# Sparse attention and a squared-ReLU MLP on one core: the second batch's loads reordered on GpSimd's queue, and a mask tile for the first batch

## The chip, the cores and the metric

The kernel runs on 1 core of one Trainium2 chip. The metric is the device time of one execution in microseconds (us). TensorE (PE) multiplies, VectorE (DVE), ScalarE (ACT) and GpSimd (POOL) work on tiles, SyncE (SP) issues transfers. Transfers issued by GpSimd and by SyncE go through two queues of descriptors to the same DMA engines.

## The reference, cut to what matters

q, k and v are [8 batches, 8 heads, 576 positions, 64]. The first four heads of each batch use a local mask, the last four a strided one; the output of attention, 4608 tokens of 512, goes through an MLP.

```python
scores = (q @ k^T) / 8
mask_local   = (rel >= 0) & (rel < 32)                         # heads 0..3, rel = i - j
mask_strided = (rel >= 0) & (pos_j % 32 == pos_i % 32)         # heads 4..7
attn = softmax(where(mask, scores, -1e9)) @ v
x = attn as [4608, 512]
out = (max(x @ w_in, 0) ** 2) @ w_out                          # w_in [512, 2048], w_out [2048, 512]
```

## The kernel before, in words

**Units and chunks.** Two heads of one batch make a unit: unit u = 4·batch + pair, pairs 0 and 1 local, 2 and 3 strided. The MLP works on chunks of 512 tokens. A chunk has 16 first matmul groups (`mm1`, L440, "MM1": four 128x512 matmuls at L448, ReLU on ScalarE at L454, square on VectorE at L455) and 16 second groups (`mm2`, L459, "MM2": four matmuls at L466). MM2 of a chunk runs over quarters of w_out: the first groups use only rows of the first quarter, `w_out(0)`, then three need `w_out(1)`, and so on.

**Steps of a unit.** `step_T` (L236) transposes q and k on TensorE (six matmuls for a local unit, eight for a strided one) and copies the result out of PSUM. `step_S` (L271) makes scores, exponentials on ScalarE (L299) and multiplications with the mask on VectorE (L305). `step_D` (L375) multiplies with v and divides by the sum of the exponentials (L406, L407). `step_E` (L410) transposes the result into `xt`, the input of MM1. From batch 2 on some of these transposes are made by DMA (`transpose_str` L158, `transpose_local` L165, L417), issued by SyncE.

**Batch 0** is written out by hand in `first_steps` (L496): a list of T, S, M (masks), N (sums and their reciprocals, L341 to L344), O (product with v), X (scaling into `xt`, L371) and P (parts of the first three MM1 groups); a number in the list is that many idle matmuls (L491). The local mask is one [128, 96] tile, broadcast over six blocks; the first block of units 0 and 1 has 32 rows set to zero by a memset (L307) after each multiplication. For strided units X reads and writes in the order (p, j).

**From batch 1 on** a planner lays attention steps among the MLP's groups. Groups have numbers (MM1 of chunk 0 is 0 to 15, MM2 of chunk 0 is 16 to 31, and so on) and weights (MM1 3, MM2 7 in the first chunks, L665 to L668). Between `g_prev` and `g_end` a batch's steps come due in proportion to the weights passed (L714 to L723). For batch 1 `g_prev` is 12 (L717) and `g_end` is 31. The attention of batch 1 has to be done before MM1 of chunk 1.

**Loads of batches 1 to 3**: `loads` (L563). SyncE's queue gets q and k of the two local units (L113), then v of all four (L185, L201). GpSimd's queue, in the order of the program, gets transfers and casts mixed. For batch 1: w_out(0), strided q and k of unit 6 (cast in the transfer, L133), casts of q and k of unit 4 (L123), w_out(1), casts of unit 5, strided q and k of unit 7, w_out(2), casts of v of the local units (L192, L193), w_out(3), casts of v of the strided units (L208). GpSimd runs these in that order, and a cast waits for SyncE's load of its source.

**Gates.** The first load of batch 1 and of batch 2 writes a tile that GpSimd first touches with a one-element copy (L112) from a weight tile (`gates`, L561): for batch 1 from the third quarter of w_in, for batch 2 from the third quarter of w_out. So SyncE starts batch 2's loads once w_out(2) has landed and GpSimd has come to that copy, behind its casts of batch 1. SyncE's queue is in program order as well.

Of the kernel before, what the change touches and what calls it, by code (L numbers as in the profile page):

```python
# [8 lines left out]
FP32 = mybir.dt.float32  # L9
BF16 = mybir.dt.bfloat16  # L10
AF = mybir.ActivationFunctionType
ALU = mybir.AluOpType

@with_exitstack
def kernel(
# [9 lines left out]
    nc = tc.nc  # L25
    B, H, S, D = q.shape
    d_model, d_ff = moe_w_in.shape
    T = B * S
# [3 lines left out]
    QL = 96  # L32
    NL = S // QL
    NJ = 8
    RH = STRIDE // NJ
    SP_ = RH * NA
# [13 lines left out]
    y_pool = ctx.enter_context(tc.tile_pool(name="y_pool", bufs=4))  # L50
# [12 lines left out]
    mask_loc = singles.tile([128, 1, QL], BF16)  # L63
    mask_str = singles.tile([SP_, 1, SP_], BF16)
# [5 lines left out]
    xt = [singles.tile([128, T], BF16, name=f"xt{p}") for p in range(4)]  # L70
# [56 lines left out]
    def load_qk_str(u):  # L127
        b, p = units[u]
        s = st.setdefault(u, {})
        for name, src in (("q", q), ("k", k)):  # L130
            t = strT.tile([128, NJ // 2, 4 * SP_], BF16, name=f"{name}T_s")
            t = t.rearrange("p a c -> p (a c)")[0:SP_, 0:2 * NJ * D].rearrange("p (h c) -> p h c", h=2)
            nc.gpsimd.dma_start(out=t, in_=src[b, 2 * p:2 * p + 2]  # L133
                                .rearrange("h (p j) d -> p h (j d)", j=NJ))
            s[name] = t
# [11 lines left out]
    XB = 2  # L147
# [67 lines left out]
    def load_w_out(i):  # L215
        c = slice(4 * i, 4 * (i + 1))
        nc.gpsimd.dma_start(out=w_out_b[:, c, :], in_=w_out_v[:, c, :])
# [53 lines left out]
    def step_S(u):  # L271
        s = st[u]
        qT, kT = s["qT"], s["kT"]
        local = is_local(u)
        w, n = (QL, NL) if local else (SP_, NJ)
        kn = 128 if local else SP_
        hn = n // 2
        e = es[u % 4]
        s["e"] = e
        banks = [[None, None], [None, None]]  # L280
        for half in range(2):
            for row in range(2):
                banks[row][half] = ps_t.tile([128, 512], FP32, name="pt")
            for i in range(hn):
                t = half * hn + i
                klo = w * t
                for row in range(2):
                    rows = slice(64 * row, 64 * row + 64)
                    if not local and units[u][0] >= XB:
                        c0 = w * (t // 4)  # L290
                        lhsT, rhs = (a[rows, t % 4, c0:c0 + w] for a in (kT, qT))
                    else:
                        lhsT, rhs = kT[rows, klo:klo + kn], qT[rows, w * t:w * (t + 1)]
                    nc.tensor.matmul(banks[row][half][0:kn, w * i:w * (i + 1)], lhsT, rhs,  # L294
                                     start=True, stop=True)

        def expo(row, half):
            lo = S * row + S // 2 * half
            nc.scalar.activation(e[0:kn, lo:lo + S // 2], banks[row][half][0:kn, 0:S // 2],  # L299
                                 AF.Exp, scale=scale)  # L300

        def masks(row):
            x = e[0:kn, S * row:S * (row + 1)].rearrange("p (t c) -> p t c", c=w)
            m = mask_loc if local else mask_str
            nc.vector.tensor_tensor(x, x, m.to_broadcast([kn, n, w]), op=ALU.mult)  # L305
            if u < 2:
                nc.vector.memset(x[0:32, 0], 0.0)  # L307

        s["masks"] = masks
        if units[u][0] == 0:  # L310
            for row, half in ((0, 0), (0, 1), (1, 0), (1, 1)):
                expo(row, half)
            return
        expo(0, 0)
        later(1, lambda: expo(0, 1), u)
        later(2, lambda: (masks(0), expo(1, 0)), u)
        later(3, lambda: expo(1, 1), u)
        later(4, lambda: masks(1), u)

    def load_v_first():  # L320
# [25 lines left out]
    def step_O(u):  # L346
        s = st.pop(u)
        e, local, i = s["e"], is_local(u), u % 2
        kn, w, hw = (128, QL, S // 2) if local else (SP_, SP_, S // 2)
        pos = []  # L350
        for half in range(2):
            po = ps_t.tile([128, 512], FP32, name="pt")
            for t in range(hw // w):
                for h in range(2):
                    if local:
                        tt = NL // 2 * half + t
                        vt, c = vl0[:, i, h, tt], S * h + w * tt
                    else:
                        vt, c = vs0[:, i, NJ * h + 2 * t + half], S * half + hw * h + w * t
                    nc.tensor.matmul(po[64 * h:64 * h + 64, w * t:w * (t + 1)], vt, e[0:kn, c:c + w],  # L360
                                     start=True, stop=True)
            pos.append(po)

        def scaled():
            for half, po in enumerate(pos):
                cols = slice(hw * half, hw * (half + 1))
                o, x, r = xt[u][:, cols], po[:, 0:hw], rv0[:, u, cols]
                if not local:
                    o = xt[u][:, 0:S].rearrange("c (p j r) -> c p j r", j=NJ // 2, r=2)[:, :, :, half]
                    x, r = (y.rearrange("c (j p) -> c p j", p=SP_) for y in (x, r))  # L370
                nc.vector.tensor_tensor(o, x, r, op=ALU.mult)  # L371

        return scaled
# [108 lines left out]
    D_ = lambda u, part: (lambda: step_D(u, part))  # L482
    E_ = lambda u: (lambda: step_E(u))

    idle_w = y_pool.tile([128, 512], FP32, name="y").bitcast(BF16)

    def warm(n):
# [8 lines left out]
    def first_steps():  # L496
        a, b, c, d = first_order
        scaled = {}

        def part(kks, ffs=range(NP)):  # L500
            for ff in ffs:
                mm1(0, ff, kks, (b, a, c, d), None if ff < 2 else ps_y)

        def masks(u):
            for row in range(2):
                st[u]["masks"](row)

        def outs(u):
            scaled[u] = step_O(u)

        for item in (("T", a, "q"), 2, ("T", a, "k"), 2, ("T", b, "q"), ("S", a), 1, ("T", b, "k"), 2, ("S", b),
                     ("M", a), 1, ("T", c, "q"), ("T", c, "k"), 1, ("N", a), ("S", c), 1, ("M", b), ("N", b), 1,
                     ("T", d, "q"), ("T", d, "k"), 2, ("S", d), 1, ("M", c), ("N", c), ("O", b), 1, ("X", b),
                     ("O", a), 1, ("M", d), ("X", a), ("N", d), ("O", c), ("X", c), ("P", (b, a), (0,)), ("O", d),
                     ("P", (b, a), (1, 2)), ("X", d), ("P", (c,)), ("P", (d,))):
            if isinstance(item, int):
                warm(item)
                continue
            op, u = item[0:2]
            if op == "T":  # L520
                step_T(u, item[2])
            elif op == "S":
                step_S(u)
            elif op == "M":
                masks(u)
            elif op == "N":
                step_N(u)
            elif op == "O":
                outs(u)
            elif op == "X":  # L530
                scaled[u]()
            else:
                part(*item[1:])
# [29 lines left out]
    def loads(b):  # L563
        u = 4 * b
        for i in range(2):
            load_qk_local(u + i, nc.sync, gate=gates.get(b) if i == 0 else None)
        for i in range(2):
            load_v_local(u + i, nc.sync)
        load_v_str(u + 2, nc.sync)
        load_v_str(u + 3, nc.sync)  # L570
        w_out = load_w_out if b == 1 else (lambda i: None)
        if b >= XB:
            cast_str_dram(b)
        w_out(0)
        if b < XB:
            load_qk_str(u + 2)
        cast_qk_local(u, pool2)
        w_out(1)
        cast_qk_local(u + 1, pool2)
        if b < XB:  # L580
            load_qk_str(u + 3)
        w_out(2)
        cast_v_local(u)
        cast_v_local(u + 1)
        w_out(3)
        cast_v_str(u + 2)
        cast_v_str(u + 3)

# [104 lines left out]
    done_prev, g_prev = 0, 0  # L693
# [20 lines left out]
    for b in range(1, B):  # L714
        g_end, s_end = ready.get(b, starts[b] - 2), ends[4 * b + 3]
        if b == 1:
            g_prev = 12  # L717
        total = sum(weights[g_prev:g_end])
        for g in range(g_prev, g_end + 1):
            due[g] = done_prev + (s_end - done_prev) * sum(weights[g_prev:g]) // total  # L720
        if b + 2 < B:
            plan(b + 2, g_end + 2, g_prev, g_end)
        done_prev, g_prev = s_end, g_end  # L723
# [41 lines left out]
```

## Time and profile before

| What | Value |
|---|---|
| Time, median of 13 runs | 317.89 us (316.56 to 319.82) |
| The profiled execution's own time | 317.94 us |
| Its span | 315.3 us |
| TensorE busy | 303.2 us (96%) |
| VectorE, ScalarE, GpSimd busy | 167.6, 162.7, 89.0 us |
| DMA | 44.4 MB, mean 141 GB/s |
| w_out, four transfers, issue to landing | 8.7 to 11.0 us |
| MM1 of chunk 0 without breaks (L448) | from 23.93 us |
| MM2 of chunk 0 (L466) | 35.67 to 61.07 us |
| TensorE's waits up to 110 us | 1.5 us for kTl copies, 1.5 us for w_out, smaller ones |

Times are counted from the start of the span; the 2.6 us between span and time lie around it. A row of a timeline has a start, a length, the engine (SPq is SyncE's queue of transfers), the line, the operation, what is written and read, the count, and in brackets how long the engine was idle before and what ended that. PEclk in the page is the clock granted to TensorE, in tenths of full speed.

### The profile page before, as it was taken

How to read it: one execution, taken by the hardware profiler on the slowest of the kernel's cores; microseconds unless marked ns; L12 is line 12 of the kernel's file. 1: busy time of each engine (PE TensorE's matmuls, PEld its weight loads, DVE VectorE, ACT ScalarE, POOL GpSimd, SP SyncE). 2: the span in 40 equal slices, each digit the busy share in tenths (PEclk: the TensorE clock that was granted, in tenths of full speed). 3: DMA queues.
4: the chain of work that ended last, by engine and by line, in shares of the span. 5: the costliest groups of instructions: out<-in, count | busy, mean ns of one | idle time of the engine just before them, and what ended most of it. 6: DMA issues, size and time to landing. Idle time of an engine off the chain costs nothing.

```text
span 315.3 us, 6218 instructions
## 1 busy us (share of the span) xinstructions
PE 303.2 (96%) x2384; PEld 149.5 (47%) x2384; DVE 167.6 (53%) x415; ACT 162.7 (52%) x337; POOL 89.0 (28%) x115
## 2 busy tenths in 40 slices
PE   7889979899999999999999999999999999999995
PEld 3444545545555544444444444444454444444442
DVE  6765544568866875577466657565455222222200
ACT  4937636578556765555555555545543444344311
POOL 8524852644840624272048015000000000000000
PEclk9979979999999999999999999999999999999999
DMA  7999999999999999999799876002111100000121
GB/s 147 148 207 223 224 202 210 208 282 217 192 216 212 175 200 205 174 239 224 143 231 222 174 160 119 33 33 54 52 45 45 45 35 34 33 35 33 51 82 67
DMA packets 86612, 44.40 MB, mean 141 GB/s; under 512 B 71032, under 2 KB 79896, under 8 KB 86392
## 3 DMA queue, kind: packets, MB, share of 16 engines
q1 hardware_dynamic: 77032, 34.09, 50.9%
q0 software_dynamic: 9408, 9.80, 19.8%
q8 instruction: 18, 0.29, 0.4%
q10 hardware_dynamic: 144, 0.13, 0.1%
q14 instruction: 10, 0.08, 0.1%
HBM read 36.70 MB, written 12.98 MB: 158 GB/s over the span
## 4 chain that ended last, share of the span: by engine, by line
PE 77%; DMA 10%; DVE 6%; SPq 3%; ACT 1%; issue 1%; POOL 1%; DVEq 0%; POOLq 0%
PE ph L448 32%; PE py L466 27%; PE ph L466 7%; DMA q_st<-in_q_dram 4%; DMA w_out_b<-in_moe_w_out_dram 3%; PE pt L294 3%; PE pt L392 3%; DMA kTl<-k_l 2%; DVE x_s L407 2%; DMA v_st<-in_v_dram 1%; PE pt L424 1%; DVE kTl L265 1%; DVE e L305 1%; PE pt L250 1%; ACT r L454 1%
## 5 line engine op out<-in xcount | busy, mean ns | idle before, releaser
L448 PE MATMUL ph<-xt,w_in_b 128*128 128x512 bf16 x572 | 144.4, 381 | 0.3 <-ACT r L454 0.3
L454 ACT ACTIVATE r<-ph 128x512 bf16<-128x512 f32 x143 | 85.3, 597 | 98.5 <-PE ph L448 97.3
L455 DVE TENSOR_TENSOR g_sb<-r 128x512 bf16<-128x512 bf16 x144 | 68.4, 477 | 104.8 <-ACT r L454 104.1
L466 PE MATMUL py<-w_out_b,g_sb 128*128 128x512 bf16 x400 | 102.8, 379 | 0.0
L466 PEld LDWEIGHTS <-g_sb 128*128 128x128 bf16 x576 | 53.1, 98 | 58.5 <-issue 2.4
L448 PEld LDWEIGHTS <-w_in_b 128*128 128x128 bf16 x576 | 51.8, 98 | 54.5 <-issue 1.0
L299 ACT ACTIVATE e<-pt 128x288 bf16<-128x288 f32 (+1 forms) x128 | 47.2, 407 | 14.5 <-PE pt L294 14.4
L466 PE MATMUL ph<-w_out_b,g_sb 128*128 128x512 bf16 x176 | 44.2, 388 | 1.5 <-DMA w_out_b<-in_moe_w_out_dram 1.5
L392 PEld LDWEIGHTS <-e 128*128 128x128 bf16 (+1 forms) x392 | 21.0, 98 | 15.7 <-issue 0.6
L192 POOL CAST vl<-vl_st 128x768 bf16<-128x768 f32 x14 | 12.6, 899 | 52.4 <-DMA vl_st<-in_v_dram 46.4
L407 DVE TENSOR_TENSOR x_s<-pt,rinv 72x384 bf16<-72x384 f32 (+1 forms) x42 | 21.4, 509 | 1.4
L123 POOL CAST q_l<-q_st 96x768 bf16<-96x768 f32 x14 | 12.5, 894 | 24.3 <-DMA q_st<-in_q_dram 24.0
L305 DVE TENSOR_TENSOR e<-e,mask_loc 128x576 bf16<-128x576 bf16 x32 | 17.5, 548 | 2.4 <-ACT e L299 2.4
L406 DVE RECIPROCAL rinv<-pt 96x6 f32<-96x6 f32 (+2 forms) x70 | 12.9, 184 | 9.0 <-PE pt L392 9.0
L305 DVE TENSOR_TENSOR e<-e,mask_str 72x576 bf16<-72x576 bf16 x32 | 16.3, 513 | 2.0 <-ACT e L299 2.0
L208 POOL CAST vs<-v_st 72x1024 bf16<-72x1024 f32 x14 | 16.3, 1181 | 3.3 <-DMA v_st<-in_v_dram 2.8
L123 POOL CAST k_l<-k_st 96x768 bf16<-96x768 f32 x14 | 13.2, 941 | 13.9 <-DMA k_st<-in_k_dram 9.1
L477 ACT COPY y<-py 128x512 f32<-128x512 f32 x25 | 14.6, 585 | 4.4 <-PE py L466 4.3
L407 DVE TENSOR_TENSOR x_l<-pt,rinv 96x384 bf16<-96x384 f32 x28 | 15.5, 553 | 1.0
L477 ACT COPY y<-ph 128x512 f32<-128x512 f32 x10 | 5.9, 585 | 17.4 <-PE ph L466 17.4
L392 PE MATMUL pt<-vs,e 72*128 72x65 bf16 x224 | 13.1, 193 | 0.0
L193 POOL CAST vl<-vl_st 32x640 bf16<-32x640 f32 x14 | 10.8, 769 | 0.9
(84 smaller groups left out, 157.6 us busy)
## 6 DMA issues: line engine op xcount, KB each, us to landing
out_dram<-y SPq DMA_DIRECT2D x35, 256.0 KB, 2.0
vl_st<-in_v_dram SPq DMA_DIRECT2D x28, 144.0 KB, 5.5
v_st<-in_v_dram SPq DMA_DIRECT2D x14, 288.0 KB
q_st<-in_q_dram SPq DMA_DIRECT2D x16, 144.0 KB, 5.4
k_st<-in_k_dram SPq DMA_DIRECT2D x16, 144.0 KB, 6.6
w_in_b<-in_moe_w_in_dram POOLq DMA_DIRECT2D x4, 512.0 KB, 12.2
w_out_b<-in_moe_w_out_dram POOLq DMA_DIRECT2D x4, 512.0 KB, 9.6
q_st<-in_q_dram SPq DMA_DIRECT2D x7, 288.0 KB, 8.5
```

Of the source, the lines that this page charges most:

```text
L123: copy(t.rearrange("p j h d -> p h j d"), s[name + "f"].rearrange("p h (j d) -> p h j d", j=6))
L208: (copy or nc.gpsimd.tensor_copy)(t[:, :, 0:D], s["vf"].rearrange("p h (j d) -> p (h j) d", d=D))
L299: nc.scalar.activation(e[0:kn, lo:lo + S // 2], banks[row][half][0:kn, 0:S // 2], AF.Exp, scale=scale)
L305: nc.vector.tensor_tensor(x, x, m.to_broadcast([kn, n, w]), op=ALU.mult)
L392: nc.tensor.matmul(po[:, n - n0, :], e[0:kn, pos(n):pos(n) + 128], rhs[0:kn, src(n), 0:D + 1], start=True, stop=True)
L406: nc.vector.reciprocal(rinv[0:w, 0:m], po[0:w, 0:m, D:D + 1])
L407: nc.vector.tensor_tensor(x, po[0:w, 0:m, 0:D], rinv[0:w, 0:m].to_broadcast([w, m, D]), op=ALU.mult)
L448: nc.tensor.matmul(ph, w_in_b[:, kk, 128 * ff:128 * (ff + 1)], xt[kk][:, 512 * c:512 * (c + 1)], start=(kk == order[0]), stop=(kk == order ...
L454: nc.scalar.activation(r, ph, AF.Relu)
L455: later(1, lambda: nc.vector.tensor_tensor(g[:, ff, :], r, r, op=ALU.mult))
L466: nc.tensor.matmul(py, g[:, ff, 128 * j:128 * (j + 1)], w_out_b[:, ff, :], start=(ff == 0), stop=(ff == 15))
L477: nc.scalar.copy(y, py)
```

## The change

1. `loads`, batch 1 only: all four pieces of w_out and both strided pairs are enqueued on GpSimd ahead of every cast, in the order w_out(0), unit 6, w_out(1), w_out(2), unit 7, w_out(3). The order among the casts, SyncE's order and batches 2 and 3 stay.
2. The planner starts batch 1's attention at group 16, the first of MM2(0), instead of group 12. `g_end` stays 31.
3. `first_steps`: a tile `mask_l0` of [128, 6, 96] with the 32 rows of the first block at zero is made once by a copy and a memset on VectorE ("Z" in the list, between scores(a) and the k transposes of b), and units 0 and 1 multiply with it; their four memsets go. It takes one more of the four buffers of `y_pool`.
4. `first_steps`: the sums of b (N) come after the transposes of d instead of before them; the idle matmuls around are split anew, with the same total.
5. X of the strided units runs in the order (j, p): PSUM and the reciprocals are read contiguously, and `xt` is written with a step of eight elements.

```diff
         def masks(row):
             x = e[0:kn, S * row:S * (row + 1)].rearrange("p (t c) -> p t c", c=w)
-            m = mask_loc if local else mask_str
-            nc.vector.tensor_tensor(x, x, m.to_broadcast([kn, n, w]), op=ALU.mult)
+            m = (mask_loc if local else mask_str).to_broadcast([kn, n, w])
             if u < 2:
-                nc.vector.memset(x[0:32, 0], 0.0)
+                m = mask_l0
+            nc.vector.tensor_tensor(x, x, m, op=ALU.mult)
...
                 if not local:
-                    o = xt[u][:, 0:S].rearrange("c (p j r) -> c p j r", j=NJ // 2, r=2)[:, :, :, half]
-                    x, r = (y.rearrange("c (j p) -> c p j", p=SP_) for y in (x, r))
+                    o = xt[u][:, 0:S].rearrange("c (p j r) -> c j p r", j=NJ // 2, r=2)[:, :, :, half]
+                    x, r = (y.rearrange("c (j p) -> c j p", p=SP_) for y in (x, r))
...
+    mask_l0 = y_pool.tile([128, 512], FP32, name="y").bitcast(BF16)[:, 0:S].rearrange("p (t c) -> p t c", c=QL)
+
+    def make_mask_l0():
+        nc.vector.tensor_copy(mask_l0, mask_loc.to_broadcast([128, NL, QL]))
+        nc.vector.memset(mask_l0[0:32, 0], 0.0)
...
-        for item in (("T", a, "q"), 2, ("T", a, "k"), 2, ("T", b, "q"), ("S", a), 1, ("T", b, "k"), 2, ("S", b),
-                     ("M", a), 1, ("T", c, "q"), ("T", c, "k"), 1, ("N", a), ("S", c), 1, ("M", b), ("N", b), 1,
-                     ("T", d, "q"), ("T", d, "k"), 2, ("S", d), 1, ("M", c), ("N", c), ("O", b), 1, ("X", b),
+        for item in (("T", a, "q"), 2, ("T", a, "k"), 2, ("T", b, "q"), ("S", a), 1, ("Z",), ("T", b, "k"), 2, ("S", b),
+                     ("M", a), 1, ("T", c, "q"), ("T", c, "k"), 1, ("N", a), ("S", c), 1, ("M", b),
+                     ("T", d, "q"), ("T", d, "k"), 1, ("N", b), 2, ("S", d), 1, ("M", c), ("N", c), ("O", b), 1, ("X", b),
...
-        w_out = load_w_out if b == 1 else (lambda i: None)
-        if b >= XB:
+        if b == 1:
+            load_w_out(0)
+            load_qk_str(u + 2)
+            load_w_out(1)
+            load_w_out(2)
+            load_qk_str(u + 3)
+            load_w_out(3)
+        else:
             cast_str_dram(b)
-        w_out(0)
-        if b < XB:
-            load_qk_str(u + 2)
         cast_qk_local(u, pool2)
-        w_out(1)
         cast_qk_local(u + 1, pool2)
-        if b < XB:
-            load_qk_str(u + 3)
-        w_out(2)
         cast_v_local(u)
         cast_v_local(u + 1)
-        w_out(3)
...
         if b == 1:
-            g_prev = 12
+            g_prev = 16
```

More of the change, by code (lines that the diff above doesn't have):

```diff
@@ L518, in first_steps @@
                 continue
-            op, u = item[0:2]
-            if op == "T":
+            op, u = (item + (None,))[0:2]
+            if op == "Z":
+                make_mask_l0()
+            elif op == "T":
                 step_T(u, item[2])
```

## The prediction, made before the changed kernel ran

> **What bounds the kernel now.** I read the busy lines of the page first, then the chain that ended last, then the waits of TensorE, then the rows of GpSimd, SyncE and TensorE in order of time where that chain leaves TensorE. The busy lines, 40 slices of 7.9 us:
>
> ```profile
> span 315.3 us, 6218 instructions
> ...
> PE   7889979899999999999999999999999999999995
> ...
> PEclk9979979999999999999999999999999999999999
> DMA  7999999999999999999799876002111100000121
> ```
>
> TensorE (PE) is full from slice 9 on. Its holes are in slices 1 to 8, and the DMA engines are full from slice 2 to about slice 20. So the early stage is a race between TensorE and the transfers. What GpSimd (POOL) issues there:
>
> ```profile
> 23.66 0.18 POOL L112 CAST q_st<-w_in_b 1x1 f32<-1x1 bf16 x1 [5.79 <-DMA w_in_b<-in_moe_w_in_dram]
> 23.90 0.76 POOL L217 DMA_DIRECT2D w_out_b<-in_moe_w_out_dram  x1
> ...
> 31.86 0.78 POOL L217 DMA_DIRECT2D w_out_b<-in_moe_w_out_dram  x1
> ...
> 35.48 0.68 POOL L133 DMA_DIRECT2D qT_s<-in_q_dram  x1
> ...
> 36.83 0.78 POOL L217 DMA_DIRECT2D w_out_b<-in_moe_w_out_dram  x1
> ...
> 41.12 0.77 POOL L217 DMA_DIRECT2D w_out_b<-in_moe_w_out_dram  x1
> ...
> 44.52 1.26 POOL L208 CAST vs<-v_st 72x1024 bf16<-72x1024 f32 x1 [0.63 <-DMA v_st<-in_v_dram]
> 47.88 0.18 POOL L112 CAST q_st<-w_out_b 1x1 f32<-1x1 bf16 x1 [2.09 <-DMA w_out_b<-in_moe_w_out_dram]
> ```
>
> The four pieces of w_out go out 8.0, 5.0 and 4.3 us apart, because each stands behind casts that wait for their own loads. The last line is the gate of batch 2's loads: it waits for the third piece. TensorE meets the second and the third piece here:
>
> ```profile
> 41.83 1.55 PE L466 MATMUL ph<-w_out_b,g_sb 128*128 128x512 bf16 x4 [1.21 <-DMA w_out_b<-in_moe_w_out_dram]
> ...
> 47.87 1.02 PE L466 MATMUL ph<-w_out_b,g_sb 128*128 128x512 bf16 x4 [0.24 <-DMA w_out_b<-in_moe_w_out_dram]
> ...
> 112.73 0.43 PE L294 MATMUL pt<-kT,kTl 64*128 64x96 bf16 x12 [0.63 <-DMA kTl<-k_l]
> ```
>
> The third line matters as much. It is scores(17), and it waits for a transpose that SyncE (SP) issued at 106.58. In SP's rows, from the gate's release
>
> ```profile
> 48.08 0.32 SPq L113 DMA_DIRECT2D q_st<-in_q_dram  x1
> ...
> 106.58 3.15 SPq L173 DMA_TRANSPOSE kTl<-k_l  x1
> ```
>
> to that one, issues stand end to end with gaps of 0.2 us at most, so a second chain runs beside TensorE from 47.88 to 112.68. Scores(16) at 103.03 was held by its transpose too (1.1 us of weight-load wait). After 113 no TensorE wait names a DMA.
>
> **What the Trainium skill says.** "DMA: Bandwidth & Descriptors", section "Issuing engines are not separate DMA queues": transfers started by different engines run on the same 16 DMA engines and interleave. The trace agrees: counting its packet records by queue, GpSimd's 1 KB packets run at about 195 a us alone (45 to 47 us) and 119 beside SP's 1.5 KB ones (28 to 30 us). Same page, "Queues, rings and completion order": an engine takes turns between rings packet by packet. So a piece enqueued earlier takes its share from SP's loads; bandwidth is not made. Same page, "Anatomy of one DMA — SWDGE (gpsimd) path": waits happen on the issuing sequencer, before dispatch. The 8.0 us between the first two pieces are such waits. "TensorE: Matmul & The Clock Gate", Part 1: after an idle window of about 3.4 us the clock is halved. The trace has granted clock 0.72 in 40 to 45 and 0.94 in 45 to 50, which is 1.7 us of lost clock.
>
> **The change, part by part.**
>
> *Order of GpSimd's queue in batch 1.* Issue times are 0.76, then 0.70 + 0.69, 0.78, 0.78, 0.68 + 0.67, 0.77, together 5.8 us, so all lie between 23.90 and 29.7. The waits these DMAs carry are for transfers landed by 27.5 (the fourth w_in piece: 11.24 + 16.3), and so cost nothing. What is queued behind them is the first q cast, 28.35 to 29.7. The k cast waits for its load until 30.98 anyway, and the 3.7 us of issue that stood between the later casts are gone, so no cast but the first is later for this.
>
> *w_out(1)*. Before, w_out(0) and the strided pair (800 packets) were through at about 33.5, and then GpSimd's queue ran nearly empty from 34.0 to 36.0 (42 packets against some 200). With the piece queued since 26 that dip goes: 160 packets at 100 to 200 a us are 0.8 to 1.6 us. Landing 41.8 becomes about 40.5. TensorE reaches it earlier: 13 groups of first matmuls at 0.865 from 23.93 end at 35.2; with 0.6 for batch 0 (below) 34.6. Three groups at 0.87, four transposes at 0.26 and scores at 0.36 follow, so it asks at 38.6 and stalls 1.9 us (1.2 before).
>
> *w_out(2)* stands ahead of the strided pair of unit 7 now: 288 packets fewer in front, 1.5 us at 190 a us to 3 at 95, beside the 0.8 to 1.6 above. Against that SP's queue now shares in 34 to 36. From 47.8 I take 45.4 (43.3 to 47). TensorE asks at 40.5 + 2.6 + 1.25 for attention = 44.4 and stalls 1.0. From there the old trace needs 61.32 − 47.87 = 13.45 to the next MM1; scores(6) and one transpose now lie behind the point, 0.66. Arrival 59.5, against 61.32: TensorE gains 1.8. The strided pair of unit 7 lands near 46.7, asked for at 46.9; w_out(3) near 49.5 against 49.7. Both are tight.
>
> *The gate* is released by the later of w_out(2) and the last v cast. SP's v loads (2304 packets of 256 bytes) had the DMA engines to themselves in 34 to 36, 1483 packets in 2 us. With GpSimd's queue full I give them 1 us more: last v load near 45.3, cast 1.26, gate 46.6, against 47.88. Bounds: 45.8 (as before) and 49.7 (rival D). So SP's chain starts 1.3 us earlier. w_out(3) has some 140 packets more to go then than before (0.7 us of work), but the DMA engines had spare time after the gate (share 0.90 in 48 to 52), so I charge 0.2: 1.1 us is left at scores(17).
>
> *Attention from MM2(0) on* (the 12 becomes 16) moves two transposes and their copies out of the last MM1 groups and packs the same steps into groups of weight 105 instead of 117 in the planner. TensorE work is the same. Of the tail, where before stalled on x_s four times (1.1 us in all), the order is almost unchanged: nothing, within ±0.5.
>
> *Batch 0.* Four memsets go (0.10 each, and the next matmul waited for the last: 0.5 at 18.40). A copy and a memset come in, into VectorE's 0.71 us hole before 8.04. The copy is bounded by 0.15 (four elements a cycle, "VectorE: DVE Perf Modes", "Mode 4×_2P") and 0.60 (one, "Mode 1× (REGULAR)"); I take 0.3. The strided outputs at L371 took 0.60 against 0.39 for the local ones; reading straight and writing with gaps saves between 0 and 0.2 each, or loses 0.1. The transposes of unit 1 come 0.7 earlier, but ScalarE is busy without a break from 10.5 to 16.9, so that is hidden. Sum 0.3 to 0.9, taken as 0.6, and hidden too: it lengthens the stall for w_out(1). If w_out(1) came by 38.6, it would count.
>
> **The sum.** TensorE is 1.8 earlier at 61, but scores(17) may start only 1.1 earlier; the remaining 0.7 turns into a longer wait there or at scores(16). The profiled run took 317.94, its span 315.3 and 2.6 around it; the median is 317.89, so they agree. 317.9 − 1.1 = 316.8.
>
> **The rivals.**
> B, SP's chain is not rigid: its issues speed up when TensorE does, or the gate comes 2.2 earlier. For it: transposes there took up to 3.15 where 1.22 is usual. Against: 65 us end to end. It gives 317.9 − 2.2 = 315.7.
> C, nothing moves: the clock halves again behind the new stalls (1.7 lost of 1.8) or the last v load holds the gate at 47.9. Then only w_out moved: 317.9. For it: the DMA engines were full anyway.
> D, slower: GpSimd's queue, full from 24 to 48, starves SP's small packets. In 36.5 to 37.0 they stood 113 to GpSimd's 64; at 226 a us their 2304 packets take 10 us instead of 5.2. Some 0.9 of the 4.8 comes back, as GpSimd's queue is then emptier; the last v load lands at 48.4, the gate falls to 49.7, and scores(17) to 112.7 + 1.8: 319.7. It decides once the v_st loads end over 1.3 us later than before. Against: the ratio comes from engines that had finished their SP share.
>
> **Numbers.** About 0.3% (0.95 us) is what can be told from no change. Likeliest case A 0.45 (315.9 to 317.4), B 0.20, C 0.17, D 0.18. Of A 0.27 lies below 316.9 and 0.18 within; with B that is 0.47 faster; C and 0.18 give 0.35 the same; D 0.18 slower. The range 315.2 to 319.3 reaches into B and D and leaves out about 0.15.
>
> **What would show it.** Right: four w_out issues within 6 us, the gate cast (L112) near 46.6, TensorE's wait for w_out near 1.9 and 1.0, and a wait on kTl near 112 that is longer than 0.63. Wrong: a gate after 47.9, v_st casts over 1.3 us late, a wait for w_out(3) or the strided pair, a second half-clock window that reaches past 50, or new waits of batch 2 between 57 and 80.

## The result, and the profile after

The changed kernel takes 322.14 us (median of 11 runs, 321.31 to 324.38), the kernel before 318.42 in the same comparison: ratio 1.0133, interval 1.0107 to 1.0158. It is slower by about 4 us, beyond the forecast range. Ratios here and below leave out executions that were markedly slower than the others of the same kernel, and in two of the experiments (old_queue, start16_only) the profiled execution was such a one, with TensorE's clock halved over 10.2 us, so its times behind that point are not compared.

The page's busy lines of the changed kernel, 40 slices of 8.0 us:

```profile
span 318.2 us, 6217 instructions
...
PE   7979979889999989999999999999999999999995
...
PEclk9969999999999999999999999999999999999999
DMA  8999993998999999999899999002100100000121
```

The seventh digit of the DMA line is new: a 3 stands where a 9 stood. It is the stretch around 50 us. GpSimd's rows there, the same lines as in the prediction:

```profile
22.76 0.18 POOL L112 CAST q_st<-w_in_b 1x1 f32<-1x1 bf16 x1 [6.00 <-DMA w_in_b<-in_moe_w_in_dram]
22.99 0.75 POOL L217 DMA_DIRECT2D w_out_b<-in_moe_w_out_dram  x1
...
25.12 1.53 POOL L217 DMA_DIRECT2D w_out_b<-in_moe_w_out_dram  x2
...
28.00 0.80 POOL L217 DMA_DIRECT2D w_out_b<-in_moe_w_out_dram  x1
...
42.03 0.99 POOL L192 CAST vl<-vl_st 128x768 bf16<-128x768 f32 x1 [6.37 <-DMA vl_st<-in_v_dram]
43.09 0.71 POOL L193 CAST vl<-vl_st 32x640 bf16<-32x640 f32 x1
46.89 1.07 POOL L192 CAST vl<-vl_st 128x768 bf16<-128x768 f32 x1 [3.08 <-DMA vl_st<-in_v_dram]
48.02 0.86 POOL L193 CAST vl<-vl_st 32x640 bf16<-32x640 f32 x1
48.94 2.13 POOL L208 CAST vs<-v_st 72x1024 bf16<-72x1024 f32 x2
51.03 0.40 POOL L112 CAST q_st<-w_out_b 1x1 f32<-1x1 bf16 x1
```

The four pieces of w_out go out within 5.8 us, as foretold. The local v loads then keep GpSimd waiting 6.37 and 3.08 us, the last four v casts stand in a row from 46.89 to 51.0, and only then comes the gate (last line), with no wait of its own: the piece that it needs had landed at 40.6. Before, the gate came at 47.88 and waited for w_out. TensorE's rows that answer to those shown before, with the new wait at 45.88, and SyncE's:

```profile
45.88 0.20 PE L392 MATMUL pt<-vl,e 128*128 128x65 bf16 x1 [1.39 <-DVE e L307]
...
105.50 0.43 PE L294 MATMUL pt<-qT,kTl 64*128 64x96 bf16 x12 [0.36 <-DMA kTl<-k_l]
115.62 0.43 PE L294 MATMUL pt<-kT,kTl 64*128 64x96 bf16 x12 [1.06 <-DMA kTl<-k_l]
```

```profile
51.45 0.32 SPq L113 DMA_DIRECT2D q_st<-in_q_dram  x1
...
110.94 1.53 SPq L173 DMA_TRANSPOSE kTl<-k_l  x1
```

No wait for w_out is left. But scores(16) and scores(17) both wait for their transposes, and scores(17) stands at 115.62 instead of 112.73: 2.9 us, which is the whole difference of the spans (318.2 − 315.3). This execution is the fastest of the eleven, and its first gate came 0.9 us earlier than before (22.76 against 23.66); from the first gate to the second it is 4.1 us longer, about what the medians differ by. From gate to scores(17) it is 64.6 us, before 64.8: SyncE's chain kept its length and started later.

Busy time by stretch, 49 to 52.5 us, in the kernel before and then in the changed one. The last columns are the granted clock, the share of the 16 DMA engines and GB/s:

```profile
49.00:52.50 3.50, 3.50 (x48) 1.89 (x46) 2.18 (x7) 1.33 (x4) 0.93 (x2) 1.00 1.00 207
```

```profile
49.00:52.50 3.50, 3.50 (x40) 2.00 (x37) 2.51 (x5) 2.03 (x5) 3.45 (x5) 1.00 0.02 3
```

The DMA engines stand still for 3.5 us, with batch 2 waiting behind a gate that GpSimd (busy 3.45 of 3.5 us) has not reached. So two theories: **the queue** (w_out's packets hold up SyncE's small v packets, the casts and the gate come late, and SyncE's chain shifts) and, since the first ReLU also came late (25.06 instead of 23.28), **the order of X** in batch 0.

The readings of all runs together. "Between" is from the first gate to the second; it is the better measure, since the first gate alone moves from 22.8 to 25.2 between these executions. "v through" is the end of the 20th packet from the last of the 2304 packets of 256 bytes, counted from the trace's packet records (the very last one ended at 38.3 before and at 46.0 in the changed kernel).

| Kernel | Gates at, us | Between | v through | scores(17), wait for kTl | Ratio to before (interval) |
|---|---|---|---|---|---|
| before | 23.7, 47.9 | 24.2 | 37.1 | 112.7, 0.63 | 1 |
| changed | 22.8, 51.0 | 28.3 | 45.6 | 115.6, 1.06 | 1.0133 (1.0107 to 1.0158) |
| queue_only | 24.2, 52.4 | 28.2 | 47.1 | 118.8, 1.12 | 1.0115 (1.0075 to 1.0154) |
| no_x_order | 23.9, 52.4 | 28.5 | 47.5 | 119.0, 1.34 | 1.0109 (1.0070 to 1.0147) |
| after_12 | 23.4, 52.1 | 28.7 | 46.5 | 117.4, 0.56 | 1.0131 (1.0082 to 1.0181) |
| late_gate | 24.5, 50.9 | 26.5 | 38.0 | 115.3, 0.37 | 1.0101 (1.0053 to 1.0149) |
| old_queue | 24.2, 47.8 | 23.7 | 37.3 | not read | 1.0012 (0.9985 to 1.0038) |
| x_order_only | 23.3, 47.9 | 24.6 | 36.6 | 113.8, none | 0.9986 (0.9963 to 1.0008) |
| batch0_masks | 24.8, 49.1 | 24.2 | 38.2 | 115.6, 0.93 | 1.0020 (0.9993 to 1.0046) |
| one_piece | 24.7, 48.4 | 23.6 | 40.9 | 113.7, none | 1.0027 (1.0004 to 1.0049) |
| early_gate | 24.0, 41.9 | 18.0 | 47.0 | 112.5, none | 1.0034 (1.0013 to 1.0055) |
| early_gate_12_p | 24.3, 42.1 | 17.8 | 47.5 | 114.7, none | 1.0050 (1.0022 to 1.0078) |
| w_out_halves | 25.2, 49.5 | 24.3 | 42.9 | 117.7, none | 1.0115 (1.0079 to 1.0152) |
| start16_only | 23.4, 47.2 | 23.8 | 36.4 | not read | none |

The times are of one execution of each kernel, the ratios of several: batch0_masks's profiled execution took 320.54 us, 1.8 above that kernel's median, and its first gate is among the latest. From scores(17) to the end of the span it is 202.6 to 203.1 us in every one of these profiles. So what makes scores(17) late, whether its transpose or TensorE, makes the whole kernel late by as much.

### The profile page after: what moved, and what is told of

It is laid out like the page before. It is cut to its first block, busy times and chain, and to the rows that moved or that the text cites. A ratio compares the mean times of both kernels' runs of the same rounds, so it can differ in the third digit from the quotient of the medians.

```text
span 318.2 us, 6217 instructions
## 1 busy us (share of the span) xinstructions
PE 303.7 (95%) x2384; PEld 149.1 (47%) x2384; DVE 177.3 (56%) x413; ACT 163.1 (51%) x337; POOL 87.9 (28%) x115
## 4 chain that ended last, share of the span: by engine, by line
PE 83%; DVE 5%; DMA 3%; ACT 3%; SPq 2%; issue 1%; POOL 1%; DVEq 0%; POOLq 0%; ACTq 0%
PE ph L448 34%; PE py L466 27%; PE ph L466 10%; PE pt L294 4%; PE pt L392 3%; PE pt L250 1%; DMA kTl<-k_l 1%; DVE g_sb L455 1%; PE pt L424 1%; SPq L173 1%; DVE x_s L407 1%; DMA q_st<-in_q_dram 1%; DMA vl_st<-in_v_dram 1%; DVE kTl L265 1%; DVE xt L371 1%
## 5 line engine op out<-in xcount | busy, mean ns | idle before, releaser
L455 DVE TENSOR_TENSOR g_sb<-r 128x512 bf16<-128x512 bf16 x144 | 73.9, 516 | 101.3 <-ACT r L454 97.4
L466 PE MATMUL ph<-w_out_b,g_sb 128*128 128x512 bf16 x176 | 42.8, 379 | 0.0
L192 POOL CAST vl<-vl_st 128x768 bf16<-128x768 f32 x14 | 13.4, 954 | 63.9 <-DMA vl_st<-in_v_dram 56.0
L123 POOL CAST k_l<-k_st 96x768 bf16<-96x768 f32 x14 | 11.8, 845 | 20.5 <-DMA k_st<-in_k_dram 17.8
L208 POOL CAST vs<-v_st 72x1024 bf16<-72x1024 f32 x14 | 15.4, 1128 | 0.4
```

Of the source, the lines that this page charges most:

```text
L123: copy(t.rearrange("p j h d -> p h j d"), s[name + "f"].rearrange("p h (j d) -> p h j d", j=6))
L192: nc.gpsimd.tensor_copy(t[:, :, :, 0:D].rearrange("p h t d -> p (h t) d"), s["vf"])
L208: (copy or nc.gpsimd.tensor_copy)(t[:, :, 0:D], s["vf"].rearrange("p h (j d) -> p (h j) d", d=D))
L455: later(1, lambda: nc.vector.tensor_tensor(g[:, ff, :], r, r, op=ALU.mult))
L466: nc.tensor.matmul(py, g[:, ff, 128 * j:128 * (j + 1)], w_out_b[:, ff, :], start=(ff == 0), stop=(ff == 15))
```

## The experiments: which edit costs the time

**queue_only**: the kernel before with the new `loads` and nothing else.

```diff
-        w_out = load_w_out if b == 1 else (lambda i: None)
-        if b >= XB:
+        if b == 1:
+            load_w_out(0)
+            load_qk_str(u + 2)
+            load_w_out(1)
+            load_w_out(2)
+            load_qk_str(u + 3)
+            load_w_out(3)
+        else:
             cast_str_dram(b)
...
```

> The kernel before with only GpSimd's queue of batch 1 reordered. Queue theory: v loads through at 44 to 45 us, gate at 50 to 51.5, no wait for w_out, scores(17) at 115 to 116, time 2 to 3 us above before. Order theory: batch 0 is as before, so the removed waits for w_out show, and the time is at or below before.

Measured 323.03 us, 1.0115: slower by as much as the whole change, within the intervals. The gate and scores(17):

```profile
52.44 0.18 POOL L112 CAST q_st<-w_out_b 1x1 f32<-1x1 bf16 x1
```

```profile
118.82 0.43 PE L294 MATMUL pt<-kT,kTl 64*128 64x96 bf16 x12 [1.12 <-DMA kTl<-k_l]
```

The gate came 28.2 us after the first one. v through, the gate and scores(17) were 2.1, 0.9 and 2.8 us later than the theory's latest. The first gate was 1.5 us later than in the changed kernel, and from gate to scores(17) it was 66.4 us instead of 64.6.

**old_queue**: the changed kernel with the old `loads`; the other four edits stay.

```diff
-        if b == 1:
-            load_w_out(0)
...
+        w_out = load_w_out if b == 1 else (lambda i: None)
...
```

> The changed kernel with GpSimd's queue of batch 1 in the order of before; mask tile, order of X, and attention from group 16 stay. Queue theory: v loads of local units through at about 37.5 us instead of 44.5, gate at 47.5 to 48.5, time at most 1 us above before. Order theory: the first ReLU stays at 25 us and the time stays 1.5 us or more above before.

Measured 319.68 us, 1.0012: no difference from before. v through at 37.3, and the gate waits for w_out again:

```profile
47.84 0.18 POOL L112 CAST q_st<-w_out_b 1x1 f32<-1x1 bf16 x1 [1.61 <-DMA w_out_b<-in_moe_w_out_dram]
```

Together with queue_only this puts the loss on GpSimd's queue, from both sides.

**x_order_only** and **no_x_order**: the kernel before with the (j, p) order of X alone, and the changed kernel without it.

```diff
-                    o = xt[u][:, 0:S].rearrange("c (p j r) -> c p j r", j=NJ // 2, r=2)[:, :, :, half]
-                    x, r = (y.rearrange("c (j p) -> c p j", p=SP_) for y in (x, r))
+                    o = xt[u][:, 0:S].rearrange("c (p j r) -> c j p r", j=NJ // 2, r=2)[:, :, :, half]
+                    x, r = (y.rearrange("c (j p) -> c j p", p=SP_) for y in (x, r))
```

> The kernel before with the (j, p) order of X as its only edit. Queue theory (GpSimd's full queue takes turns packet by packet with SyncE's 256-byte packets, so batch 2's gate comes 3 us late): GpSimd's queue is untouched, gate at 47.5 to 48.3 us, time within 0.3% of before. Order theory (each strided multiplication costs 1.3 us instead of 0.6 and holds up batch 0): the first ReLU comes at 25.1 instead of 23.3, the wait for w_out(1) shrinks from 1.2 to 0, and the time is 0.5 to 1.8 us above before.

> The changed kernel with X back in the (p, j) order. Queue theory: gate still at 50 to 51.5 us, scores(17) still near 115.5, time 2 to 3 us above before. Order theory: the first ReLU comes at 23 us or earlier and the time falls by 1.5 to 2.9 us against the changed kernel, to at most 1.4 us above before.

X itself, in the changed kernel and then in no_x_order, for the first strided unit (two multiplications in a row):

```profile
15.37 2.73 DVE L371 TENSOR_TENSOR xt<-pt,g_sb 128x288 bf16<-128x288 f32 x2 [0.99 <-PE pt L360]
```

```profile
16.00 1.20 DVE L371 TENSOR_TENSOR xt<-pt,g_sb 128x288 bf16<-128x288 f32 x2 [0.99 <-PE pt L360]
```

The new order makes each multiplication 1.37 us instead of 0.60. In x_order_only the first ReLU came at 26.04 and MM2(0) began at 38.43, 2.8 us later than before. Not all of that is the order of X: TensorE's clock was halved there from 19.2 to 26.1, before only from 18.3 to 21.7, which is up to 1.7 us more. In old_queue, after_12 and early_gate, which have this order, the other edits of batch 0 and one such window of 3.4 us, the first ReLU came at 24.0 to 24.3, 0.7 to 1.0 us later than before. Yet the time of x_order_only is the same (0.9986): no wait for w_out is left there, MM1 of chunk 1 starts at 62.39 against 61.32, and scores(17) finds its transpose ready at 113.8. And without it the changed kernel stays at 1.0109, within the interval of the whole change. So the edit is bad by itself, and hidden: the order theory is right about batch 0 and wrong about the end.

**after_12**: the changed kernel with `g_prev = 12`.

> The changed kernel with attention of batch 1 from group 12 as before. Queue theory: v loads and gate as in the changed kernel (44 to 47.5 and 50 to 52.5 us), time within 1 us of the changed kernel, 3 to 4.5 us above before. Dense theory (packing the attention into MM2(0) costs the time): the time falls by 1.5 us or more.

Measured 322.51 us, 1.0131, the same as the changed kernel within the intervals. The dense theory does not explain the loss.

**start16_only**: the kernel before with `g_prev = 16`.

> The kernel before with attention of batch 1 starting at group 16 as its only edit. Hidden: MM2(0) starts 0.5 us earlier, the wait for w_out(1) grows by as much, the gate stays at 47.9, the time is within 0.3% of before. Dense: transposes, scores and product with v of one unit come closer together, new waits for masks of 1 to 2 us appear in MM2(0); if TensorE sets the end there, the time rises by up to 1.5 us.

Inconclusive. One of six runs took 318.39 us, the others 323.7 to 325.5, and the profiled one of these has the clock halved from 42.8 to 53.0, behind a wait of 2.1 us for w_out(1) that ended at 41.4. Why this kernel fell into it in five of six runs is open. old_queue, which has the same start at 16, had most of its runs between 317.9 and 320.9.

**batch0_masks**: the kernel before with the mask tile and the moved sums.

> The kernel before with the mask tile and the moved sums of b as its only edits. First ReLU 0.3 to 0.9 us earlier than 23.3; the wait for w_out(1) grows by as much and the time is within 0.3% of before. If batch 0 is not hidden, the time is 0.3 to 0.9 us below.

Measured 318.73 us, 1.0020, the interval holds 1. The first ReLU came 1.6 us earlier (21.67), more than I had thought, and the wait for w_out(1) grew to 3.2 us. What batch 0 gained here was waited away. That the gain comes from the mask tile is not shown: this execution had no halved clock in batch 0, where before has 3.4 us of it (1.7 us lost), and in early_gate_12_p, with the same two edits of batch 0 and such a window, the first ReLU came at 23.29, as before.

## The experiments: how the queue costs it

**w_out_halves**: the changed kernel with GpSimd's w_out packets half as long.

```diff
-        nc.gpsimd.dma_start(out=w_out_b[:, c, :], in_=w_out_v[:, c, :])
+        for m in (slice(0, 256), slice(256, 512)):
+            nc.gpsimd.dma_start(out=w_out_b[:, c, m], in_=w_out_v[:, c, m])
```

> The changed kernel with each piece of w_out as two transfers of 256 columns, so that GpSimd's packets are 512 bytes instead of 1024 and the bytes are the same. Turn theory (the engines take one packet of each queue in turn): SyncE's 256-byte packets, 76 to 78 per half us in the changed kernel, rise to 110 to 150, the v loads of local units end at 40 to 42.5 us instead of 45.6, the gate comes at 48 to 50 and the time is 1 to 3 us below the changed kernel. Bandwidth theory (queues share by bytes, or the DMA engines are simply full): the 256-byte packets stay at 76 per half us or fall, the gate stays at 50 to 52, and the time stays.

Packets that ended in the half us from each given time, while both queues are full, counted from the packet records of the two kernels:

```
                     GpSimd            SyncE
changed, 36.0        74 of 1024 B      77 of 256 B
changed, 37.5        77 of 1024 B      71 of 256 B
changed, 42.5        73 of 1024 B      78 of 256 B
w_out_halves, 37.0  124 of  512 B     122 of 256 B
w_out_halves, 39.5  121 of  512 B     122 of 256 B
```

Close to one to one in both, though the sizes differ. Halving GpSimd's packets raised SyncE's rate from about 77 to about 120 and brought v through at 42.9, 0.4 us past the forecast; the time between the gates fell from 28.3 to 24.3, and no transpose is waited for at scores(17). So the turn theory holds and the bandwidth theory falls. The time did not follow (1.0115, against a forecast of 1 to 3 us below the changed kernel). GpSimd stood still for 1.7 and 1.6 us ahead of two issues, as nowhere in the changed kernel, so its q and k casts came as late as 37.7 to 40.3. TensorE waited for them and for masks:

```profile
38.55 0.43 PE L251 MATMUL pt<-ident,q_l 96*128 96x96 bf16 x6 [0.93 <-POOL q_l L123]
...
47.75 0.20 PE L393 MATMUL pt<-vl,e 128*128 128x65 bf16 x1 [2.05 <-DVE e L308]
```

Its clock was halved from 48.4 to 51.8 as well, and MM1 of chunk 1 began at 65.8, 3.5 us later than in the changed kernel. In this execution TensorE sets the end. That the doubled number of transfers made GpSimd stand still is likely but not shown.

**late_gate**: the kernel before with batch 2's gate on the fourth piece of w_out.

```diff
-    gates = {1: w_in_b[0:1, 0, 1024:1025], 2: w_out_b[0:1, 8, 0:1]}
+    gates = {1: w_in_b[0:1, 0, 1024:1025], 2: w_out_b[0:1, 12, 0:1]}
```

> The kernel before with the gate of batch 2's loads on the fourth piece of w_out instead of the third; nothing else moves, no load of batch 1 is later. Chain theory (from the gate on SyncE's issues run end to end and set when scores(17) may start): gate at 50.0 to 51 us instead of 47.9, scores(17) at 114.5 to 116 with a wait for its transpose over 0.6 us, time 1.5 to 3 us above before. If SyncE's chain can catch up, scores(17) stays near 112.7 and the time within 0.3% of before.

The gate and scores(17), rows of GpSimd and of TensorE:

```profile
50.91 0.18 POOL L112 CAST q_st<-w_out_b 1x1 f32<-1x1 bf16 x1 [4.86 <-DMA w_out_b<-in_moe_w_out_dram]
```

```profile
115.26 0.43 PE L294 MATMUL pt<-kT,kTl 64*128 64x96 bf16 x12 [0.37 <-DMA kTl<-k_l]
```

With all loads of batch 1 on time (v through at 38.0) and the gate alone 3.0 us later than before, scores(17) is 2.5 us later and the time 320.94 us, 1.0101. Its wait is shorter than foretold, since TensorE also lost 2.5 us at w_out(2) in this execution and its clock was halved from 48.7 to 52.1; TensorE by itself would have come to scores(17) only 0.4 us earlier. So it is less this profile than the time over six runs, with the gate as the only edit, that shows it: the lateness of the gate is enough to make most of the loss.

**early_gate**: the changed kernel with the gate ahead of the v casts; the v loads stay late.

```diff
         cast_qk_local(u + 1, pool2)
+        if b == 1:
+            t = early[u + 4, "q"] = qk_st.tile([QL, 2, 6 * D], FP32, name="q_st")
+            nc.gpsimd.tensor_copy(t[0:1, 0, 0:1], gates.pop(2))
         cast_v_local(u)
...
```

> The changed kernel with the one-element copy that gates batch 2's loads moved on GpSimd's queue ahead of batch 1's v casts; everything else stays, the late v loads too. Order theory (the loss is the 3.9 us in which no packet moves between batch 1's last load and batch 2's first, since the gate stands behind the v casts): the gate comes at 41 to 43 us, the packets run on without a gap, scores(17) comes at 113 or earlier, and the time is within 1 us of before. Work theory (mixing the queues costs the DMA engines throughput): the gap closes, but the time stays 2 us or more above before.

GpSimd's rows around the gate, and the stretch that was empty:

```profile
41.91 0.18 POOL L595 CAST q_st<-w_out_b 1x1 f32<-1x1 bf16 x1 [5.74 <-DMA w_out_b<-in_moe_w_out_dram]
...
48.26 0.83 POOL L195 CAST vl<-vl_st 128x768 bf16<-128x768 f32 x1 [4.35 <-DMA vl_st<-in_v_dram]
```

```profile
49.00:52.50 3.50, 2.88 (x39) 1.67 (x37) 2.27 (x6) 1.86 (x5) 3.38 (x5) 1.00 1.14 250
```

The v loads end later still (47.0), but batch 2's loads stand behind them in SyncE's queue: the DMA engines move 250 GB/s where they moved 3. The time is 318.98 us, 1.0034: about three quarters of the loss is back by moving one element's copy. So the DMA engines did not lose the work; the gate's place lost it. What makes up the last quarter stays open: scores(17) waits for no transpose there.

**one_piece**: the kernel before with only w_out(1) ahead of the first casts.

> The kernel before with only w_out(1) moved ahead of the first casts; w_out(2), w_out(3) and the strided pair of unit 7 keep their places. Turn theory: about 500 of the 2304 small v packets go at 77 per half us while w_out(1) drains, the rest at full rate; the v loads end at 38 to 39.5 us instead of 37.1, the gate, which waits for w_out(2), stays within 1 us of 47.9, the wait for w_out(1) goes, and the time is within 0.3% of before. If any piece moved up is enough to starve the v loads, the gate comes at 49.5 or later and the time is 1.5 us or more above before.

Measured 319.04 us, 1.0027, v through at 40.9, 1.4 us beyond the forecast, since the first gate was late and the small packets first went one to one (153 of them to 154 of GpSimd's in the us from 36). The gate interval is 23.6. TensorE's wait for w_out did not go: 2.1 us, now for the third piece.

**early_gate_12_p**: early_gate with attention from group 12 and the old order of X.

> early_gate with attention from group 12 and X in the (p, j) order: the changed queue, the early gate, the mask tile and the moved sums are left. Order theory: time within 0.5 us of before or up to 1 us below, since the waits for w_out are gone and batch 2's loads are not late. If late v casts alone hold TensorE, products with v of units 4 and 5 wait 2 to 4 us and the time is 1 to 3 us above before.

Measured 319.73 us, 1.0050, which is the second forecast and not the first. Products with v wait 1.5 and 0.6 us for GpSimd's v casts, and one transpose 1.2 us for x_s. Batch 0 was no earlier than in the kernel before. No version was found that is faster than the kernel before.

## Why the prediction was wrong, point by point

*What bounds the kernel* was read rightly: SyncE's chain from the gate to scores(17) is what a load order has to serve. Late_gate shows it: from gate to gate it takes 2.2 us more than before, and the ratio is 1.0101.

*The step that failed* is "With GpSimd's queue full I give them 1 us more: last v load near 45.3, cast 1.26, gate 46.6". From the 20th small packet to the 20th from the last it took 12.1 us (33.5 to 45.6) instead of 4.5, so the local v was 8.5 us late, not 1; the last v load, of larger packets, ended at 49.0; and as the last four v casts then stood in a row, the gate came at 51.0. I had quoted the Trainium skill, "DMA: Bandwidth & Descriptors", "Queues, rings and completion order", that an engine changes rings packet by packet, and drew from it that a piece "takes its share"; I then gave v 1 us more without a count behind it. In the changed kernel's packet records the two queues come out one to one in count (from 29 to 44 us, 2231 packets of GpSimd's to 2235 of SyncE's), so the queue with 256-byte packets gets a fifth of the bytes beside one with 1024-byte packets. The sum was within reach: 2304 packets against 2624 of GpSimd's at one each, as long as both last. The 5.2 us of before were measured with GpSimd's queue nearly empty from 34 to 36, which I had noticed and booked only as a gain for w_out(1).

*Rival D* named the right mechanism and the right side, with 0.18. Its ratio (113 to 64) was read from a half us in which the mix was turning over (the one before had 266 to 28, the one after 25 to 89); one to one would have given 2304 / 153 a us = 15 us and a gate past 50. So the rival ended at 319.7, and the range with it at 319.3. The 15 us are more than the measured 12.1, as GpSimd's queue ran out near 44 and the last 650 small packets went in 2 us. *Rival B*, that SyncE's chain can catch up, fell: 64.6 us from gate to scores(17) against 64.8, and 64 to 67 us in every run in which scores(17) waits for its transpose. *Rival C*'s second half-clock window was not seen in the changed kernel's profile; the one in batch 0 was twice as long (6.8 us).

*w_out*: the direction was right, the size too small. The second, third and fourth piece landed at 37.0, 40.6 and 46.5 (forecast 40.5, 45.4 and 49.5): GpSimd's queue had the engines' turns that v lacked. The waits of 1.9 and 1.0 us did not come. The 8.0 us between the first two issues of before, put down to waits of the transfers, were 4.0 us of waits of the two casts between them; the rest was issues and the casts themselves.

*TensorE* was to reach MM1 of chunk 1 at 59.5 and did at 62.37. MM2(0) started at 36.93, not 34.6. The slow X and the longer halved clock of batch 0 are both in that, and the profile does not part them. Its length was as forecast (25.4 against 24.9), but with other waits: 1.39 at 45.88, where the product with v of unit 4 came 3.8 us after its scores and its second mask wasn't done, and five of 0.3 to 0.5. Whether *attention from MM2(0) on* costs TensorE more than the ±0.5 stays open: from group 12, after_12 waits 0.8 and 0.7 us for v casts instead. At the end it made no difference (after_12).

*Batch 0*: the copy took 0.30 us, as chosen. X was bounded at a loss of 0.1 each and lost 0.77 each; I had looked at the reads and not at the writes. That batch 0 is hidden held in both directions: a first ReLU 2.8 us later (x_order_only) and 1.6 earlier (batch0_masks), whatever made it so, left the time where it was.

## What to carry to other kernels

Where two DMA queues are full, count packets and not bytes: here they went one to one, and the queue with the small rows starved. Before moving a transfer earlier, list what shares the engines with it and whether that other load carries a gate; here 8.5 us of lateness in one load went through casts into a one-element copy, which came 3 us late, and from there into a chain of 65 us. A gate on an in-order queue waits for everything ahead of it, so its place counts as much as its condition.

## What the runs showed of the hardware that was not expected

- With both queues full, the counts of packets were equal over long stretches, once the packets of 4 bytes are counted too: 2231 of GpSimd's to 2235 of SyncE's in the changed kernel from 29 to 44 us, 982 to 979 in queue_only from 36 to 42, 1346 to 1342 in w_out_halves from 36 to 41.5. It held for rows of 1024 beside 256 bytes, 512 beside 256, and 1024 beside 1536 (391 to 390 in the changed kernel from 29 to 32.5). It did not hold everywhere: the kernel before has 238 to 194 from 28 to 30 us. How many packets make one turn, such counts do not show.
- Writing 288 bf16 results with a step of 16 bytes took 1.37 us on VectorE, although both sources were read contiguously; with a step of 4 bytes and both sources strided it took 0.60, all contiguous 0.41. Which of the steps is at fault was not tried apart.
- The halved clock came in windows of 3.4 us, one, two or three in a row: 18.3 to 21.7 and 42.2 to 45.6 before, 18.2 to 25.1 in the changed kernel, 42.8 to 53.0 in start16_only. The prediction speaks of an idle window of about 3.4 us ahead of it; here TensorE was busy for part of the 3.4 us ahead of each of these stretches: 1.97 and 1.83 us before, 1.98 in the changed kernel, 1.30 in start16_only.
